# Probabilities loaded batch by batch, and the scaling of the joint slots' softmax on ScalarE

## The chip, the cores and the metric

The kernel runs on one core of a Trainium2 chip. The metric is the device time of one execution in microseconds (us). Three runs of the kernel before took 1032.5, 1033.79 and 1034.16 us; the median is 1033.79 us.

## What is computed

The inputs are q, k and v of 4 batches, 8 heads, 576 tokens and 64 columns, in fp32, a memory matrix and a vector for each batch and head, a gate for each head, and for each of the 2304 tokens four domain probabilities. In short:

```
scores = q @ k.T / 8, causal; a = softmax(scores)
phi(x) = max(x, exp(x) - 1 where x <= 0) + 1
x = g * (phi(q) @ M) / (phi(q) . z + 1e-6) + (1 - g) * (a @ v)      g = sigmoid(beta) per head
p = probs / (probs.sum(-1) + 1e-9)                                  per token, four experts
out = sum over e of p[:, e] * (relu(x @ w1[e]) @ w2[e])             512 -> 1024 -> 512
```

## The kernel before

**Tiles and stages.** Tokens are cut in chunks of 128 (the fifth chunk of a batch has 64). Chunks 0 and 1 of a batch are done together for a pair of heads ("joint" tasks), chunks 2 to 4 in tasks of their own. The expert part works on nine groups of 256 tokens. Group 0 is batch 0, chunks 0 and 1, which `first_run` computes alone at the start, in an order written out by hand (`ORDER`). After it the expert part runs in phases (half an expert each, 40 in all). A phase is four pieces of `mm1` (h = x·w1, four fc), each followed by relu into hh on ScalarE (L767) and the rest hl on VectorE (L768), then `mm2` (y = h·w2) for each tile of 128 tokens, whose result VectorE adds to acc with the token's probability as factor (L802, L804). Every fp32 product is three matmuls of rounded parts: high times high, and the two mixed ones. Phases 0 to 4 have one group, so 256 columns in mm1; from phase 5 on two groups share a phase (but in the last three), so 512 columns.

**Weights.** SyncE (SP) loads weight blocks into four buffers stg. `w_prep` makes the two parts of one block: the high part (w1h, or w2h) is copied by ScalarE at L205 for w1, and in phases 0 to 4 and the last four for w2 too; the low part (w1l, w2l) is a subtraction on GpSimd (POOL) at L209. When it is done the next block is loaded into the same buffer. Where a phase's mm1 piece has been evicted, w_prep makes one w2 block of the same phase; after each tile of mm2, w1 blocks of the next phase (two at a time in phases 0 to 4).

**Slots.** The attention of the other tasks is cut in steps with a slot number and a priority; sorted by these, they give one fixed list. A joint task has four slots. In its even slots it does the scores (`j_qk`: matmuls L421, mask and maximum L426 on VectorE), the exponentials with row sums (`j_exp`, L440, ScalarE) and the transposed probabilities of the slot before (`j_pt`: transposes L309, pth on ScalarE L480, ptl on VectorE L481). In its odd slots `j_norm` (priority -0.5, so the first of the slot) takes the two row sums (one per head), adds 1e-9 and multiplies with 1 + exp(beta) at L453, inverts at L456 and scales the exponentials at L458, all on VectorE. There are 24 joint slots; half have rows of 128 columns a head (chunk 0), half 256 (chunk 1).

Steps for tasks to come lie between. In a task's slot 1 (its first odd one) the queries of the next task are transposed (tq) and split: `split_q`, qa and qb on ScalarE (L317, L318), then the other halves on VectorE (L319, L322). In its last odd slot `t_phi1` does the ex operations of a task two ahead (L281, L282, ScalarE), and at the start of a task's first slot `t_trk` splits the next task's keys (kha, khb L329 on ScalarE, kl L331 on VectorE) and copies them across by DMA (`dup_k`, L336). At the end of a task's first slot `t_phi3` (L300 to L304, VectorE) normalises phi(q) of the next task and writes qp; in the task's second even slot `t_trqp` transposes its own qp (tp) and splits it (qpa, qpb).

**Order.** Each engine executes its instructions in the order in which the program issues them. How the list of steps is laid between the matmul pieces is a planner's choice: each step has a cost (400 without matmuls; 1500 and its matmul time with them), and before each mm piece steps are issued until their summed cost reaches a target that rises with the work done. The target is a line from the start to the steps that a group must have; it is steeper for the first groups.

**Probabilities.** `c_probs` (L729 to L738) is called once, in `first_run` after the weight step w3 and the steps up to slot -8. It loads the probabilities into the tile pn with eight DMAs of SP's queue: for each of four batches one of 8 KB (four full chunks) and one of 1 KB (the chunk of 64). `c_probs2` (L740 to L746, a step of slot -3 with priority 20) normalises all 18 columns of pn with four VectorE operations. Phase 0's first use of pn is the acc operation at L802.

Of the kernel before, what the change touches and what calls it, by code (L numbers as in the profile page):

```python
# [10 lines left out]
AF = mybir.ActivationFunctionType  # L11
ALU = mybir.AluOpType
AX = mybir.AxisListType
# [36 lines left out]
def tile_attention_moe(  # L50
# [13 lines left out]
    nc = tc.nc  # L64
    P = 128
    B, H, S, D = q.shape
    NT, DM = out.shape
    E, _, F = w1.shape
# [36 lines left out]
    def ctile(shape, dt, name):  # L105
        return cst.tile(shape, dt, tag=name, name=name)
# [15 lines left out]
    ebp = ctile([P, H], F32, "ebp")  # L122
    gate = ctile([P, H], F32, "gate")
    pn = ctile([P, NT // P, E], F32, "pn")
    psm = ctile([P, NT // P], F32, "psm")
# [65 lines left out]
    def w_prep(i, kind, pool=False):  # L191
        last_ = i >= PHASES - 4
        act = (kind == "1" or i < START[1] or last_) and not pool
        j = wpos["prep"]
        if j >= len(wseq) or wseq[j][0] != i or wseq[j][1] != kind:
            return
        wpos["prep"] += 1
        fc = wseq[j][2]
        t = stg.pop(j)
        hi, lo = (w1s if kind == "1" else w2s)[fc]  # L200
        if kind == "1":
            hi = hi.rearrange("p c f -> p (c f)")
            lo = lo.rearrange("p c f -> p (c f)")
        if act:
            nc.scalar.activation(hi, t, AF.Copy)  # L205
        else:
            nc.gpsimd.tensor_scalar(hi, t, 1.0, 1.0, ALU.mult, ALU.mult)  # L207
        dve = (last_ and fc % 2) or (i < START[1] and fc < PR["lod"])
        (nc.vector if dve else nc.gpsimd).tensor_tensor(lo, t, f(hi), ALU.subtract)  # L209
        w_dma()  # L210
# [179 lines left out]
    for t in tasks:  # L390
# [7 lines left out]
        for hds, c in order:  # L398
            s = Slot()
# [49 lines left out]
    def j_norm(i):  # L449
        s = slots[i]  # L450
        h = 2 * s.t.a
        r = s.st[:, 4:6]
        nc.vector.scalar_tensor_tensor(  # L453
            r, s.st[:, 2:4], 1e-9, ebp[:, h : h + 2], ALU.add, ALU.mult
        )
        nc.vector.reciprocal(r, r)  # L456
        for hd in range(2):
            nc.vector.tensor_scalar(  # L458
                s.s3[:, hd], s.s3[:, hd], r[:, hd : hd + 1], None, ALU.mult
            )  # L460

    def j_pt(i):
# [199 lines left out]
    def ev(slot, prio, fn, cost=0.0):  # L662
        events.setdefault(slot, []).append((prio, len(events.get(slot, [])), fn, cost))
# [21 lines left out]
    for i, s in slots.items():  # L685
        w = wid(s.c)
        t = s.t
        if t.joint:
            ev(i, PQ["qk"], lambda i=i: j_qk(i), 4 * mm(w))
            ev(i, PQ["exp"], lambda i=i: j_exp(i))  # L690
            ev(i + PQ["jn"][0], PQ["jn"][1], lambda i=i: j_norm(i))
            ev(i + PQ["jp"][0], PQ["jp"][1], lambda i=i: j_pt(i), 218.0 * (s.c + 1))
            if i in t.end:
                ev(i + PQ["jo"][0], PQ["jo"][1], lambda i=i: j_o(i), 6 * mm(GW) + 4 * mm(P))
            continue
        ev(i, PQ["qk"], lambda i=i: s_qk(i), 2 * mm(w) if w <= 512 else 6 * mm(w // 2))
        ev(i, PQ["exp"], lambda i=i: s_exp(i))
        ev(i + 1, PQ["norm"], lambda i=i: s_norm(i))
        ev(i + 2, PQ["pt"], lambda i=i: s_pt(i), 109.0 * min(s.c + 1, 4))
        if s.c == 4:  # L700
            ev(i + 2, PQ["pt"] + 0.1, lambda i=i: s_pt(i, True), 109.0)
        if i in t.end:
            cost = mm(t.nq) + sum(2 * mm(t.nq - max(0, j * P - t.q0)) for j in range(t.nk))
            ev(i + 3, PQ["o"], lambda i=i: s_o(i), cost)

    ev(-3, 20, lambda: c_probs2())
    steps = []
    for sl in sorted(events):
        es = sorted(events[sl], key=lambda e: (e[0], e[1]))
# [16 lines left out]
        b, c = pieces[0]  # L726
        return 4 * b + c if c < 4 else 4 * B + b // 2

    def c_probs():  # L729
        for b in range(B):  # L730
            nc.sync.dma_start(
                out=pn[:, 4 * b : 4 * b + 4],
                in_=probs[b * S : b * S + 4 * P].rearrange("(t p) e -> p t e", p=P),
            )
            nc.sync.dma_start(
                out=pn[(b % 2) * D : (b % 2) * D + D, 4 * B + b // 2],
                in_=probs[b * S + 4 * P : (b + 1) * S, :],
            )  # L738

    def c_probs2():  # L740
        nc.vector.tensor_reduce(psm, pn, AX.X, ALU.add)
        nc.vector.tensor_scalar(psm, psm, 1e-9, None, ALU.add)
        nc.vector.reciprocal(psm, psm)
        nc.vector.tensor_tensor(
            pn, pn, psm.unsqueeze(2).to_broadcast([P, NT // P, E]), ALU.mult
        )  # L746

    acc = {}
# [90 lines left out]
    def first_run():  # L839
        b = FIRST[0]  # L840
# [200 lines left out]
        def f_w(j):  # L1041
            w_prep(0, "1" if j < HF else "2", True)
            if j in (1, 3):
                while si[0] < len(steps) and steps[si[0]][0] <= (-9 if j == 1 else -8):
                    run_step()
            if j == 3:
                c_probs()

        def f_d(j):
            z_ = moe_bank(f"id{j}")  # L1050
# [26 lines left out]
        for j in range(2):  # L1077
            o = slice(j * D, (j + 1) * D)
            nc.sync.dma_start(out=mbd[o, :, o], in_=m4[j])
        nc.scalar.activation(ebp, betab, AF.Exp)  # L1080
        nc.scalar.activation(gate, betab, AF.Exp, scale=-1.0)
        nc.vector.tensor_scalar(ebp, ebp, 1.0, None, ALU.add)
# [41 lines left out]
    with tc.manual_schedule():  # L1124
        si = [0]

        def run_step():
            steps[si[0]][2]()
            si[0] += 1

        last_mask()
        for i in range(2):
            nc.gpsimd.memset(f(QK[i]["qz"]), 0.0)
            nc.gpsimd.memset(f(QK[i]["qa"][:, 3 * P :]), 0.0)
        first_run()
        phases = [phase_parts(i) for i in range(PHASES)]
        pcost = [sum(c for c, _ in ph) for ph in phases]
# [66 lines left out]
```

## Time and profile before

| | |
|---|---|
| three runs, median | 1033.79 us |
| the profiled execution | 1030.5 us |
| its span, first to last instruction | 1028.6 us |
| PE busy | 1006.3 us (98%) |
| VectorE (DVE) busy | 680.9 us (66%) |
| ScalarE (ACT) busy | 487.5 us (47%) |
| GpSimd (POOL) busy | 574.9 us (56%) |
| mean granted TensorE clock | 0.993 |

The profile is of one execution. Its own time, 1030.5 us, is 1.9 us more than its span and 3.3 us less than the median of the runs. The chain of work that ended last runs over PE for 87% of the span; the remaining PE idle time is 22 us. By slices of a fortieth of the span, PE's busy share is under 9 tenths only in the first, second, fourth and fifth (up to some 129 us) and the last. VectorE's is 8 tenths or more from the third to the eleventh, where the joint tasks run. A granted clock of 1.00 is 2.4 GHz, 0.50 is 1.2 GHz.

### The profile page before, as it was taken

What the parts mean: (1) busy time and instruction counts of PE and PEld (TensorE: products, weight loads), DVE (VectorE), ACT (ScalarE), POOL (GpSimd) and SP (SyncE); (2) the same over time, 40 slices, a digit from 0 to 9 for tenths busy, and PEclk for the clock granted to TensorE, in tenths of its full rate; (3) what the DMA queues carried; (4) which work ended last, traced back from release to release, by engine and by line L of the source; (5) the groups of instructions that cost most, each with busy time, mean ns of one, the idle gap of its engine ahead of it and who ended that gap; (6) DMA issues with size and microseconds to landing.
All of it is one profiled execution on the core that took longest, in us unless ns stands there. A gap on an engine that the chain in (4) does not pass through costs nothing.

```text
span 1028.6 us, 16265 instructions
## 1 busy us (share of the span) xinstructions
PE 1006.3 (98%) x5202; PEld 845.7 (82%) x5202; DVE 680.9 (66%) x1634; ACT 487.5 (47%) x1156; POOL 574.9 (56%) x557
## 2 busy tenths in 40 slices
PE   8798899999999999999999999999999999999998
PEld 5687788888888888888888888888888888888887
DVE  6588888888877776877687867766665323222344
ACT  7476756555555545544554555445444222211243
POOL 6476766666654465456554555565653645656233
PEclk9899999999999999999999999999999999999999
DMA  6566554464434444445434454353231432433254
GB/s 149 125 170 172 146 152 112 131 167 120 131 100 111 127 120 111 114 121 138 107 95 106 139 139 120 82 153 105 81 102 58 131 95 82 126 100 98 76 143 134
DMA packets 213669, 123.16 MB, mean 120 GB/s; under 512 B 100688, under 2 KB 187728, under 8 KB 213584
## 3 DMA queue, kind: packets, MB, share of 16 engines
q1 hardware_dynamic: 213440, 122.12, 44.0%
q8 instruction: 42, 0.69, 0.3%
q14 instruction: 43, 0.35, 0.1%
q10 hardware_dynamic: 144, 0.00, 0.0%
HBM read 106.86 MB, written 4.72 MB: 108 GB/s over the span
## 4 chain that ended last, share of the span: by engine, by line
PE 87%; DVE 4%; POOL 3%; issue 2%; ACT 1%; SPq 1%; DMA 1%; POOLq 0%; DVEq 0%; ACTq 0%
PE y L788 36%; PE h L758 35%; PE sp L547 4%; PE pt L309 4%; PE o L648 4%; POOL w1l L209 1%; POOL w2l L209 1%; PE tk L309 1%; PE tq L309 1%; PE tp L309 1%; PE sp L421 1%; PE o L495 0%; DMA kha<-kha 0%; ACT s L440 0%; PE o L643 0%
## 5 line engine op out<-in xcount | busy, mean ns | idle before, releaser
L209 POOL TENSOR_TENSOR w1l<-stg,w1h 128x512 fp32r<-128x512 f32 x152 | 198.4, 1317 | 315.4 <-ACT w1h L205 260.8
L758 PE MATMUL h<-xh,w1h 128*128 128x512 f32 (+1 forms) x640 | 248.0, 388 | 0.0
L758 PE MATMUL h<-xh,w1l 128*128 128x512 f32 (+1 forms) x640 | 237.3, 371 | 0.4 <-POOL w1l L209 0.4
L788 PE MATMUL y<-w2h,hh 128*128 128x512 f32 x576 | 237.6, 413 | 0.0
L758 PE MATMUL h<-xl,w1h 128*128 128x512 f32 (+1 forms) x640 | 236.3, 369 | 0.0
L788 PE MATMUL y<-w2h,hl 128*128 128x512 f32 x576 | 227.2, 394 | 4.2 <-DVE hl L768 4.2
L788 PE MATMUL y<-w2l,hh 128*128 128x512 f32 x576 | 226.5, 393 | 0.6 <-POOL w2l L209 0.6
L209 POOL TENSOR_TENSOR w2l<-stg,w2h 128x512 fp32r<-128x512 f32 x152 | 199.3, 1314 | 44.6 <-ACT w2h L205 34.0
L767 ACT ACTIVATE hh<-h 128x512 fp32r<-128x512 f32 (+1 forms) x160 | 88.9, 556 | 242.3 <-PE h L758 240.6
L768 DVE SCALAR_TENSOR_TENSOR hl<-h,hh 128x512 fp32r<-128x512 f32 (+1 forms) x160 | 101.9, 637 | 123.0 <-ACT hh L767 121.9
L804 DVE SCALAR_TENSOR_TENSOR acc<-y,pn,acc 128x512 f32<-128x512 f32 x126 | 94.3, 748 | 73.3 <-PE y L788 72.1
L758 PEld LDWEIGHTS h<-xh,w1l 128*128 128x128 f32 x640 | 120.8, 189 | 22.0 <-POOL w1l L209 0.6
L758 PEld LDWEIGHTS h<-xh,w1h 128*128 128x128 f32 x640 | 121.2, 189 | 16.3
L758 PEld LDWEIGHTS h<-xl,w1h 128*128 128x128 f32 x640 | 121.5, 190 | 15.7
L788 PEld LDWEIGHTS y<-w2h,hl 128*128 128x128 f32 x576 | 108.9, 189 | 30.3 <-DVE hl L768 6.1
L788 PEld LDWEIGHTS y<-w2l,hh 128*128 128x128 f32 x576 | 109.7, 190 | 19.0 <-POOL w2l L209 1.6
L788 PEld LDWEIGHTS y<-w2h,hh 128*128 128x128 f32 x576 | 109.3, 190 | 18.0
L590 ACT ACTIVATE pth<-pt 128x384 fp32r<-128x384 f32 (+3 forms) x128 | 50.6, 421 | 108.1 <-PE pt L309 107.7
L205 ACT ACTIVATE w1h<-stg 128x512 fp32r<-128x512 f32 x156 | 93.8, 625 | 9.6 <-DMA stg<-in_moe_w_dram 8.1
L207 POOL TENSOR_SCALAR w2h<-stg 128x512 fp32r<-128x512 f32 x128 | 82.0, 641 | 15.8 <-PE y L788 15.7
L309 PE MATMUL pt<-ident,s 128*128 128x128 f32 (+1 forms) x376 | 61.2, 274 | 0.4 <-DVE s L458 0.4
L555 DVE CUSTOM_DVE_ANT_0 s<-sp,mask 128x384 f32<-128x384 f32 (+1 forms) x96 | 52.9, 563 | 12.6 <-PE sp L547 11.8
(157 smaller groups left out, 1411.6 us busy)
## 6 DMA issues: line engine op xcount, KB each, us to landing
stg<-in_moe_w_dram SPq DMA_DIRECT2D x320, 256.0 KB, 2.9
natall<-in_k_dram SPq DMA_DIRECT2D x34, 128.0 KB, 2.8
out_dram<-acc SPq DMA_DIRECT2D x16, 256.0 KB, 2.0
natall<-in_v_dram SPq DMA_DIRECT2D x32, 128.0 KB, 2.5
natall<-in_q_dram SPq DMA_DIRECT2D x60, 64.0 KB, 2.7
kha<-kha SPq DMA_DIRECT2D x16, 128.0 KB, 3.0
khb<-khb SPq DMA_DIRECT2D x16, 128.0 KB, 2.6
natall<-in_k_dram SPq DMA_DIRECT2D x28, 64.0 KB, 2.4
```

Of the source, the lines that this page charges most:

```text
L205: nc.scalar.activation(hi, t, AF.Copy)
L207: nc.gpsimd.tensor_scalar(hi, t, 1.0, 1.0, ALU.mult, ALU.mult)
L209: (nc.vector if dve else nc.gpsimd).tensor_tensor(lo, t, f(hi), ALU.subtract)
L309: nc.tensor.transpose(dst, src, ident[0:n, 0:n])
L547: nc.tensor.matmul(pt[:, 0 : b_ - a], lhsT=q_, rhs=qk[k_][:, a:b_], start=y == 0, stop=y == len(pairs) - 1,)
L555: nc.vector.tensor_tensor_reduce(s.s[:, a:b_], pt[:, 0 : b_ - a], mask[:, m0 : m0 + b_ - a] if c < 4 else mask4[:, a:b_], 1.0, 3.0e38, ALU ...
L590: nc.scalar.activation(dh, src, AF.Copy)
L758: nc.tensor.matmul(pt[0][:, cols], lhsT=w_[:, c], rhs=x_[:, c, cols], start=(c == 0 and z == 0), stop=(c == NKD - 1 and z == 2),)
L767: nc.scalar.activation(h_, pt[0][:, cols], AF.Relu)
L768: nc.vector.scalar_tensor_tensor(l_, pt[0][:, cols], 0.0, f(h_), ALU.max, ALU.subtract)
L788: nc.tensor.matmul(pt[0], lhsT=h_[fc][:, tk], rhs=w_, start=(fc == 0 and z == 0), stop=(fc == HF - 1 and z == 2),)
L804: nc.vector.scalar_tensor_tensor(acc[g, tt], pt[0], pe, acc[g, tt], ALU.mult, ALU.add)
```

## The change

The scaling of the joint slots' exponentials (L458) goes from VectorE to ScalarE, in place in the program. The one operation on both row sums, which reads two tiles of two columns (L453), becomes two operations on one column each, with the head's factor as a per-row scalar operand. Batch 0's probabilities are loaded right after the memory matrices early in `first_run`, those of batches 1 to 3 in slots 2, 6 and 10, and the four short chunks in slot 14. The normalisation of pn is split: the four columns of batch 0 in slot -3, the other 14 columns in slot 16. Each of these is the last of its slot (priority 20). The five added steps have a planner's cost of 400 each. Nothing else is altered.

```diff
@@ j_norm
         r = s.st[:, 4:6]
-        nc.vector.scalar_tensor_tensor(
-            r, s.st[:, 2:4], 1e-9, ebp[:, h : h + 2], ALU.add, ALU.mult
-        )
+        for hd in range(2):
+            nc.vector.tensor_scalar(
+                r[:, hd : hd + 1],
+                s.st[:, 2 + hd : 3 + hd],
+                1e-9,
+                ebp[:, h + hd : h + hd + 1],
+                ALU.add,
+                ALU.mult,
+            )
         nc.vector.reciprocal(r, r)
         for hd in range(2):
-            nc.vector.tensor_scalar(
-                s.s3[:, hd], s.s3[:, hd], r[:, hd : hd + 1], None, ALU.mult
+            nc.scalar.activation(
+                s.s3[:, hd], s.s3[:, hd], AF.Copy, scale=r[:, hd : hd + 1]
             )
@@ list of steps
-    ev(-3, 20, lambda: c_probs2())
+    ev(-3, 20, lambda: c_probs2(0, 4))
+    for i, b in enumerate(range(1, B)):
+        ev(4 * i + 2, 20, lambda b=b: c_probs((b,)))
+    ev(14, 20, lambda: c_tails())
+    ev(16, 20, lambda: c_probs2(4, NT // P))
@@ loads and normalisation of pn
-    def c_probs():
-        for b in range(B):
+    def c_probs(bs):
+        for b in bs:
             nc.sync.dma_start(
                 out=pn[:, 4 * b : 4 * b + 4],
                 in_=probs[b * S : b * S + 4 * P].rearrange("(t p) e -> p t e", p=P),
             )
+
+    def c_tails():
+        for b in range(B):
             nc.sync.dma_start(
                 out=pn[(b % 2) * D : (b % 2) * D + D, 4 * B + b // 2],
                 in_=probs[b * S + 4 * P : (b + 1) * S, :],
             )
-    def c_probs2():
-        nc.vector.tensor_reduce(psm, pn, AX.X, ALU.add)
...
+    def c_probs2(c0, c1):
+        p_, m_ = pn[:, c0:c1], psm[:, c0:c1]
+        nc.vector.tensor_reduce(m_, p_, AX.X, ALU.add)
...
@@ first_run
-            if j == 3:
-                c_probs()
...
             nc.sync.dma_start(out=mbd[o, :, o], in_=m4[j])
+        c_probs((b,))
         nc.scalar.activation(ebp, betab, AF.Exp)
```

## Rows read from the trace of the kernel before

**Rows 1.** PE around 44 us: start, length, engine, line, what, [idle before, releaser].

```profile
43.96 0.44 PE L421 MATMUL sp<-kha,qa 128*128 128x128 f32 x1 [6.04 <-DMA kha<-kha]
```

**Rows 2.** Busy by stretch: PE, PEld, DVE, ACT, POOL (count); PEclk, DMA, GB/s.

```profile
44.00:49.20 5.20, 5.20 (x20) 4.69 (x21) 1.99 (x10) 1.44 (x6) 0.00 (x0) 0.50 0.02 4
...
52.31:68.66 16.35, 14.79 (x103) 12.95 (x101) 13.66 (x34) 12.18 (x32) 12.09 (x12) 1.00 0.59 162
...
86.80:90.20 3.40, 3.40 (x11) 2.62 (x10) 2.77 (x10) 2.82 (x9) 0.00 (x0) 0.50 0.63 187
...
125.00:1000.00 875.00, 873.94 (x4382) 733.12 (x4381) 574.74 (x1337) 392.41 (x900) 484.22 (x462) 1.00 0.42 114
```

**Rows 3.** SP's queue from 31 to 39 us, in order of time.

```profile
31.48 0.62 SPq L731 DMA_DIRECT2D pn<-in_moe_domain_probs_dram  x1
...
36.61 2.18 SPq L184 DMA_DIRECT2D stg<-in_moe_w_dram  x4
38.89 0.50 SPq L336 DMA_DIRECT2D kha<-kha  x1
```

**Rows 4.** ScalarE before the first joint scores.

```profile
34.00 0.38 ACT L329 ACTIVATE khb<-tk 64x256 fp32r<-64x256 f32 x1
```

**Rows 5.** PE's late matmuls in phases 1 to 4, in order of time.

```profile
68.18 0.50 PE L788 MATMUL y<-w2h,hl 128*128 128x512 f32 x1 [1.56 <-DVE hl L768]
...
85.53 0.51 PE L788 MATMUL y<-w2h,hl 128*128 128x512 f32 x1 [2.42 <-DVE hl L768]
...
102.80 0.50 PE L788 MATMUL y<-w2h,hl 128*128 128x512 f32 x1
...
117.95 0.66 PE L309 MATMUL tp<-ident,qp 128*128 128x128 f32 x2 [2.29 <-DVE qb L322]
```

**Rows 6.** ScalarE in the same phases, in order of time.

```profile
57.39 0.39 ACT L767 ACTIVATE hh<-h 128x256 fp32r<-128x256 f32 x1
...
60.28 0.40 ACT L440 ACTIVATE s<-s,st 128x128 f32<-128x128 f32 x1 [0.98 <-DVE st L426]
...
62.33 0.37 ACT L317 ACTIVATE qa<-tq 64x256 fp32r<-64x256 f32 x1
...
63.41 0.62 ACT L205 ACTIVATE w2h<-stg 128x512 fp32r<-128x512 f32 x1
...
72.17 0.41 ACT L281 ACTIVATE ex<-natall 128x256 f32<-128x256 f32 x1
...
73.73 0.38 ACT L767 ACTIVATE hh<-h 128x256 fp32r<-128x256 f32 x1
...
92.97 0.39 ACT L767 ACTIVATE hh<-h 128x256 fp32r<-128x256 f32 x1 [1.09 <-PE h L758]
...
108.41 0.38 ACT L767 ACTIVATE hh<-h 128x256 fp32r<-128x256 f32 x1 [0.27 <-PE h L758]
```

**Rows 7.** VectorE and POOL in the cycle of 57 to 73 us.

```profile
61.68 0.69 DVE L481 TENSOR_TENSOR ptl<-pt,pth 128x512 fp32r<-128x512 f32 x1 [0.88 <-ACT pth L480]
...
64.82 1.26 DVE L453 SCALAR_TENSOR_TENSOR st<-st,ebp 128x2 f32<-128x2 f32 x1
...
71.94 0.75 DVE L804 SCALAR_TENSOR_TENSOR acc<-y,pn,acc 128x512 f32<-128x512 f32 x1 [0.24 <-PE y L788]
...
60.78 5.29 POOL L209 TENSOR_TENSOR w2l<-stg,w2h 128x512 fp32r<-128x512 f32 x4
```

**Rows 8.** Single lines: count, duration in ns (least/median/most), first and last start.

```profile
L453 DVE SCALAR_TENSOR_TENSOR st<-st,ebp x24: 149/582/1264, 49.2 to 238.1; 128x2 f32<-128x2 f32 x24
...
L458 DVE TENSOR_SCALAR s<-s,st x48: 273/347/1559, 49.5 to 240.2; 128x128 f32<-128x128 f32 x24, 128x256 f32<-128x256 f32 x24
...
L584 DVE TENSOR_SCALAR st<-st,ebp x80: 198/205/211, 249.0 to 787.8; 128x1 f32<-128x1 f32 x80
...
L946 ACT ACTIVATE sf<-sf,stf x16: 387/448/508, 8.7 to 27.8; 128x128 f32<-128x128 f32 x8, 128x256 f32<-128x256 f32 x8
```

**Rows 9.** The operations of `c_probs2` in their stretch: DVE, ACT busy, PEclk, DMA, GB/s.

```profile
38.30:39.45 1.15, 0.90 (x4) 0.00 (x0) 1.00 1.09 329
```

More of the change, by code (lines that the diff above doesn't have):

```diff
@@ L738, in c_probs @@
             )
-    def c_probs2():
-        nc.vector.tensor_reduce(psm, pn, AX.X, ALU.add)
-        nc.vector.tensor_scalar(psm, psm, 1e-9, None, ALU.add)
-        nc.vector.reciprocal(psm, psm)
+    def c_probs2(c0, c1):
+        p_, m_ = pn[:, c0:c1], psm[:, c0:c1]
+        nc.vector.tensor_reduce(m_, p_, AX.X, ALU.add)
+        nc.vector.tensor_scalar(m_, m_, 1e-9, None, ALU.add)
+        nc.vector.reciprocal(m_, m_)
         nc.vector.tensor_tensor(
-            pn, pn, psm.unsqueeze(2).to_broadcast([P, NT // P, E]), ALU.mult
+            p_, p_, m_.unsqueeze(2).to_broadcast([P, c1 - c0, E]), ALU.mult
         )
```

## The prediction

> **What bounds the kernel now.** I read the busy times by stretch first, then what PE waited for, then the queues of the engines around each wait. Past 125 us PE is the bound: from 125 to 1000 it is busy for 873.94 of 875 us at a granted clock of 1.00 [rows 2]. A change can gain 1.1 us there and can lose more. The time to be had lies before: one wait of 6.04 us at 43.96 for the key copy kha [rows 1], after which 44.0 to 49.2 runs at a clock of 0.50 [rows 2], and once in each of phases 1 to 4 a late matmul, at 68.18, 85.53, about 102.8 and 117.95, with 1.56, 2.42 and 2.29 us before the first, second and fourth [rows 5]. The 2.42 too is followed by half clock, from 86.8 to 90.2 [rows 2]. The reader is to see that these are two different limits: the first is SP's queue, the others a ring through ScalarE, VectorE, POOL and PE.
>
> **The loads leave SP's queue.** The eight probability loads take SP from 31.48 to 36.61, 5.13 us, and the weight loads and kha stand behind them [rows 3]. Without them kha waits for its data, which ScalarE has at 34.38 [rows 4], so it goes at about 34.4, not 38.89. It took 43.96 - 38.89 = 5.07 us from issue to PE's start; with the same here PE starts at 39.5, 4.5 us earlier. The floor of the gain is 0 (the 1 MB of weights ahead of it land no sooner), the ceiling 6.04. I take 4.5, as the transfers ahead go out earlier with it. The wait left is 1.5 us; a wait of 1.56 lies in a stretch at 1.00 [rows 5, 2], so I also take back half of the 5.2 us at half clock, 2.6. Together -7.1 us.
>
> Batch 0's load is moved past SP's first weight loads, where I cost it at 0, and at 0.62 at most, its issue [rows 3]; it is needed only by the acc operation. The loads of batches 1 to 3 and the four short ones issue beside SP's weight loads of phases 0 to 3, which mostly wait for POOL; 0 us, and at most 7 x 0.62 = 4.3 if each delayed a copy that PE waits for (the row of kha shows that such a case exists). The split normalisation adds four operations in slot 16: 0.9 us as the four take now [rows 9], on VectorE, right before that slot's sums. I take 0.9 into cycle 4; the least is 0, the most 2.2 (each of two may wait as long as L453's longest, 1.26 less its least 0.15, but only one has POOL to wait for as a rule). The five steps add 2000 to the planner's sum before slot 18, some 2% of it; pieces shift by one matmul piece at most. 0 us, at most 1.5 either way (three y matmuls of 0.50 [rows 5]).
>
> **The sums and the scaling.** On VectorE L453 goes (24 of 149 to 1264 ns, median 582) for 48 like L584, which takes 198 to 211 ns in all 80 of its cases, and L458 goes, 48 of 273 to 1559 [rows 8]. So VectorE gets some 2 to 3 us back per task. That is worth nothing by itself unless VectorE ends the wait, so I ask who ends it after.
>
> ScalarE takes the scaling in its place in the program, ahead of the next qa (odd slot 1) and ahead of ex (odd slot 3). It must wait there for VectorE's reciprocal, and everything behind waits with it: hh, the w2h and w1h copies, so POOL's w2l, so PE. No row here shows this wait; I build it from rows of the cycle at 57 to 74 us. A pair of scalings is 0.7 us (128 columns) and 0.9 (256): one takes 0.387 to 0.508 [rows 8], and two lie between full overlap (0.4, 0.5) and end to end (0.8, 1.0); I am nearer the latter, since qa to the end of w2h, four operations, takes 64.03 - 62.33 = 1.7 without a gap [rows 6].
>
> *From hh to PE's late matmul.* ScalarE does hh, w2h, hh, w2h (2 x 0.9), the exponentials and the transposed block up to ptl: 61.68 - 60.28 = 1.4 [rows 6, 7]. From ptl to the sums VectorE takes 64.82 - 61.68 = 3.14 [rows 7]; the two new sums and the reciprocal 0.7 (three like L584 [rows 8]). ScalarE, free at 62.33 [rows 6], would stand until 65.5. Then the pair, 0.7, qa to w2h, 1.7, and POOL's last w2l, 5.29 / 4 = 1.32 [rows 7]. In all 1.8 + 1.4 + 3.14 + 0.7 + 0.7 + 1.7 + 1.3 = 10.7 us; before it was 68.18 - 57.39 = 10.8 [rows 5, 6]. So VectorE's gain is spent: PE now waits for w2l in place of hl.
>
> *From there to the next hh.* Before: 73.73 - 68.18 = 5.55 us [rows 5, 6]. After, ex starts not at 72.17 [rows 6] but behind acc (71.94, next operation 0.66 later, an estimate from 0.75 less the overlap), sums and reciprocal 0.7 and the pair 0.9: 74.2. That is +2.0 on all that follows.
>
> *Clock.* PE has 14.8 us of work in a cycle of 16.35 [rows 2]. With 2 us more it waits over 3, longer than the 2.42 that was followed by 3.4 us at half clock. PE is then later with the y that acc needs: +1.5 of the 1.7 lost in cycles that did not have it.
>
> The four cycles, PE's late matmul to the next:
> Cycle 1 (phase 0's slots 0 to 3, and up to 68.18) has both pairs, 1.6 us; the wait at the first, the 65.5 - 62.33 = 3.1 above less the ptl (0.7) that slot 0 has not, 2.4; the 0.7 of sums and reciprocal at the second; less the idle 0.98 before the exponentials at 60.28 [rows 6], which takes some of it up: hh comes 3.7 later against PE's own start, and hh to PE is 10.7 for 10.8: +3.6.
> Cycle 2: +2.0, +1.5 for the clock, and 10.7 for 85.53 - 73.73 = 11.8: +2.4.
> Cycle 3 (it had half clock already): 5.55 + 2.0 + 1.5 = 9.05 for 92.97 - 85.53 = 7.44, +1.6. In slot 12 the third hh stands behind the scaling too, with its w2h and the two evictions of o: 0.62 and three like the 0.37 of qa [rows 6], 1.7 more; one hh and w2h fewer, 0.9, lie before the exponentials, which I let wait 0.6 for the mask: 12.1 for 102.8 - 92.97 = 9.8, +2.3. Together +3.9.
> Cycle 4: +2.0, +1.5 for the clock; and up to tp, which waits for VectorE's qb: 1.5 and 1.4 to ptl, 3.14 to the sums, 0.9 of the split normalisation, sums 0.7, pair 0.7, qa and its partner on ScalarE 0.8, the same on VectorE 0.9 (an estimate): 10.0 for 117.95 - 108.41 = 9.5, +0.5. Together +4.0.
> Past 125 us ScalarE is busy for 392.41 of 875 us [rows 2] and copies no w2; I take the new waits as hidden by its idle time, and half of PE's 1.1 us of waits as gone: -0.5. If that cover fails, seven tasks by 1 us cost 7.
>
> Sum: -7.1 + 3.6 + 2.4 + 3.9 + 4.0 - 0.5 = +6.3 us. On the profiled execution's own 1030.5 us that is 1036.8; the median of the runs is 3.3 higher, which gives 1040.1.
>
> The Trainium skill bears on the first link. Perfetto Trace Analysis, section "Tensor Engine Instruction (MATMUL, LD_WEIGHTS)", calls ScalarE and VectorE strict FIFO. By that rule no copy behind the scaling can slip past it, and the sum stands; were it otherwise, the four cycles would cost nothing and -7.6 would be left. The rows so far show no operation that passes a waiting one.
>
> **Rivals.** *VectorE's relief is what counts* (faster). If ScalarE's stand is covered by the time in which it waits for PE anyhow, the waits of rows 5 shrink. All of them gone is -6.3, with their two half-clock stretches of 1.7 each -3.4; half of that with the -7.1 is -12, none of it -7.1; I take -8: 1026. For it: VectorE is the engine named at each of those waits, and L453 waits up to 1.1 us beyond its least. Against: w2l comes after the scaling, and ScalarE is busy 12.18 us of 16.35 in a cycle already. It decides if ScalarE stands under 1 us at the scaling.
> The Trainium skill, SBUF — State Buffer, section "SBUF: two separate sides", says that GpSimd and a VectorE operation of two SBUF inputs, or in a two-port mode, exclude each other for a whole instruction. By that rule the waits in L453 and L458 do go, and this rival gets its chance; rows 8 bear it out with L584's even 198 to 211 ns.
>
> *The clock holds.* The cycles lengthen but PE keeps full clock: without the 1.5 in cycles 2 to 4, 6.3 - 4.5 = +1.8: 1035.6.
>
> *The first gap stays.* kha lands no earlier, since the transfers ahead of it need the time: half of the 7.1 is lost, 6.3 + 3.5 = +9.8: 1043.6. For it: the transfer took 5 us for a small copy. Against: with the loads gone the weights ahead go out sooner.
>
> **Chances.** The forecast 0.50 (its own range 1036 to 1044), VectorE's relief 0.28, the clock holds 0.12, the first gap stays 0.10. A measurement of this kernel tells 0.2%, 2.1 us, from no change. Slower takes 0.47 of the forecast and all of the last, 0.57; within 0.2% the third, 0.12; faster the second and the forecast's tail, 0.31. The range goes from the relief's -8 to +12: 1026 to 1046, which leaves some 0.12 below and 0.07 above.
>
> **What would show it.** In the profile after, the wait before the first joint scores is 1 to 2 us and the stretch behind it at full clock (first step). ScalarE has idle time of some 3 us before the scaling in slots 4, 8 and 12, ended by VectorE's reciprocal (second). PE's waits in phases 1 to 4 end on POOL's w2l, not on hl, and are 3 us or more, with half clock after (third). Past 125 us PE's waits stay near 1 us. The prediction is wrong if ScalarE's idle time at the scaling is under 1 us, if PE's waits up to 125 us sum to less than before, or if the gap at the first scores is still 5 us.

## The result, and the profile after

The changed kernel takes 1039.8 us (median of 6 runs, 1038.4 to 1042.53), the kernel before in the same series 1033.97 us (6 runs, 1032.5 to 1035.12). The ratio is 1.0059, 95% interval 1.0043 to 1.0074: slower, where 1040.1 was forecast. The profiled execution took 1038.49 us, span 1036.6 us (before 1028.6), mean granted clock 0.997 (before 0.993). So the two profiles lie 8.0 us apart, the medians 5.8. PE is busy for 870.42 us between 125 and 1000 us (before 873.94 [rows 2]).

First the largest wait of any engine after, between 40 and 260 us (who waited, for whom: us in total, times, longest):

```profile
ACT s L464 <- DVE st L462: 49.2, 24, 4.1
```

It is new: ScalarE stands at each of the 24 pairs of scalings for VectorE's reciprocal, 2.05 us on average. PE's own waits over the whole span, same columns:

```profile
PE y L802 <- POOL w2l L209: 4.8, 5, 1.6
PE tk L309 <- DMA natall<-in_k_dram: 4.6, 4, 1.6
PE y L802 <- ACT w2h L205: 4.5, 3, 1.8
PE tp L309 <- DVE qb L322: 3.4, 2, 3.1
PE sp L421 <- DMA kha<-kha: 1.7, 1, 1.7
```

The wait for kha shrank from 6.04 us [rows 1] to 1.7. Where PE's mm2 waited for VectorE's hl [rows 5], it now waits for w2h and w2l, which stand behind the scaling on ScalarE and POOL. PE in order of time after; 39.74 answers to [rows 1], the y and tp lines to [rows 5]:

```profile
39.74 0.30 PE L421 MATMUL sp<-kha,qa 128*128 128x128 f32 x1 [1.67 <-DMA kha<-kha]
52.26 0.41 PE L309 MATMUL tk<-ident,natall 128*128 128x128 f32 x2 [1.59 <-DMA natall<-in_k_dram]
...
63.61 0.49 PE L802 MATMUL y<-w2h,hh 128*128 128x512 f32 x1 [1.12 <-ACT w2h L205]
64.98 0.50 PE L802 MATMUL y<-w2l,hh 128*128 128x512 f32 x1 [0.88 <-POOL w2l L209]
...
81.67 0.49 PE L802 MATMUL y<-w2h,hh 128*128 128x512 f32 x1 [1.58 <-ACT w2h L205]
83.03 0.50 PE L802 MATMUL y<-w2l,hh 128*128 128x512 f32 x1 [0.87 <-POOL w2l L209]
...
99.70 0.50 PE L802 MATMUL y<-w2h,hh 128*128 128x512 f32 x1 [1.80 <-ACT w2h L205]
101.06 0.51 PE L802 MATMUL y<-w2l,hh 128*128 128x512 f32 x1 [0.86 <-POOL w2l L209]
...
120.06 0.41 PE L309 MATMUL tp<-ident,qp 128*128 128x128 f32 x2 [3.06 <-DVE qb L322]
124.58 0.50 PE L802 MATMUL y<-w2l,hh 128*128 128x512 f32 x1 [1.57 <-POOL w2l L209]
```

The late matmuls of phases 1, 2 and 4 start at 64.98, 83.03 and 120.06, where before they started at 68.18, 85.53 and 117.95: 3.2 and 2.5 us ahead, then 2.1 us behind. At the end of the span PE is 8.0 us behind. So 5.9 us were lost past the fourth cycle. ScalarE around one stand, after (to be held against [rows 6]):

```profile
54.48 0.39 ACT L781 ACTIVATE hh<-h 128x256 fp32r<-128x256 f32 x1
...
57.60 0.63 ACT L205 ACTIVATE w2h<-stg 128x512 fp32r<-128x512 f32 x1
61.27 0.70 ACT L464 ACTIVATE s<-s,st 128x128 f32<-128x128 f32 x2 [3.03 <-DVE st L462]
61.87 0.36 ACT L317 ACTIVATE qa<-tq 64x256 fp32r<-64x256 f32 x1
...
62.93 0.62 ACT L205 ACTIVATE w2h<-stg 128x512 fp32r<-128x512 f32 x1
...
72.61 0.38 ACT L781 ACTIVATE hh<-h 128x256 fp32r<-128x256 f32 x1
```

ScalarE has nothing to do but wait for 3.03 us, while qa, hh and w2h stand behind. The w2h for which PE waits at 63.61 is the one that starts right after.

### The profile page after: what moved, and what is told of

The parts are those of the page before. It is cut to its first block, busy times and chain, and to the rows that moved or that the text cites. A ratio compares the mean times of both kernels' runs of the same rounds, so it can differ in the third digit from the quotient of the medians.

```text
span 1036.6 us, 16307 instructions
## 1 busy us (share of the span) xinstructions
PE 1007.7 (97%) x5202; PEld 843.9 (81%) x5202; DVE 652.9 (63%) x1614; ACT 503.7 (49%) x1204; POOL 572.1 (55%) x557
## 4 chain that ended last, share of the span: by engine, by line
PE 82%; issue 4%; POOL 4%; ACT 3%; DVE 3%; DMA 2%; SPq 1%; POOLq 0%; ACTq 0%; DVEq 0%
PE h L772 34%; PE y L802 34%; PE sp L553 4%; PE o L654 3%; PE pt L309 3%; POOL w2l L209 2%; POOL w1l L209 1%; PE tk L309 1%; DMA kha<-kha 1%; SPq L263 1%; PE tq L309 1%; PE tp L309 1%; ACT s L440 1%; DMA natall<-in_k_dram 0%; PE o L649 0%
## 5 line engine op out<-in xcount | busy, mean ns | idle before, releaser
L292 POOL TENSOR_TENSOR rl<-qp,zb 128x384 f32<-128x384 f32 (+1 forms) x28 | 25.1, 895 | 64.5 <-DVE qp L288 58.8
```

## The experiments

Every ratio is against the kernel before in runs of the same series. Its median was 1033.48 to 1034.48 us in these series, so a difference between kernels of different series is good to about 1 us. "In place" is the changed kernel's place for the scaling, right behind the sums and the reciprocal.

| scaling of the joint slots | loads of before | later loads |
|---|---|---|
| VectorE, sums of before | 1033.5 (the kernel before) | 1031.9 |
| VectorE, one-input sums | 1030.5 | 1030.5 |
| ScalarE, in place | 1046.6 | 1039.8 (the changed kernel) |
| ScalarE, later in the slot | 1026.9 | 1021.0 |

**The loads alone.** The later loads and the split normalisation with the sums and scaling of before:

```diff
 (changed kernel; j_norm as before the change)
-            nc.scalar.activation(s.s3[:, hd], s.s3[:, hd], AF.Copy, scale=r[:, hd : hd + 1])
+            nc.vector.tensor_scalar(s.s3[:, hd], s.s3[:, hd], r[:, hd : hd + 1], None, ALU.mult)
```

> The loads and the split normalisation as in the change, the sums and the scaling as before. Queue theory (ScalarE stands at the scaling and all behind it is late; the loads only gain): the wait before the first joint scores falls from 6.0 to 1.7 us and PE keeps the 4.2 to 4.9 us that the changed kernel has gained at its first tp, so 1028 to 1031 us. Rival (the moved loads and the split normalisation cost on the way what they gain at the start): 1033 to 1037 us, and the ScalarE part alone is harmless.

Measured: 1031.93 us, ratio 0.9989 (0.9977 to 1.0001). The wait for kha is down to 1.7 us as expected, but the gain of 2.5 to 5.5 us that the queue theory gives is not there: PE's later waits, in the columns used above, are

```profile
PE y L796 <- DVE hl L776: 6.1, 3, 2.8
PE tp L309 <- DVE qb L322: 4.7, 1, 4.7
```

against 4.2 and 2.3 us before. Against the kernel before PE is ahead by 6.4 us at the first tp and by 0.8 at the fifth (tp is the transpose of qp, done once a task; its starts serve as milestones below). Where VectorE ends PE's waits, PE started earlier only waits longer here.

**The normalisation alone.** The loads of before with the changed `j_norm`:

```diff
 (kernel before)
-            nc.vector.tensor_scalar(s.s3[:, hd], s.s3[:, hd], r[:, hd : hd + 1], None, ALU.mult)
+            nc.scalar.activation(s.s3[:, hd], s.s3[:, hd], AF.Copy, scale=r[:, hd : hd + 1])
```

> The sums and the scaling as in the change, the loads as before. Queue theory: PE loses what the changed kernel lost after its first tp, some 2 us in each of phases 1, 3 and 4 and 6 us past 125 us, on top of the kernel before: 1043 to 1048 us, with ScalarE standing some 45 to 50 us in all before the scaling. Rival (the relief of VectorE pays, and the loads are what costs): 1028 to 1034 us.

Measured: 1046.62 us, ratio 1.0124 (1.0109 to 1.0139), as the queue theory has it: the normalisation costs 13.1 us and the loads then bring 6.8. Part of both is clock: the mean granted clock is 0.988 to 0.989 in these runs and 0.992 to 0.998 in those of the changed kernel.

**The sums alone.** The kernel before with the two one-input sums, scaling on VectorE:

```diff
 (kernel before)
-        nc.vector.scalar_tensor_tensor(r, s.st[:, 2:4], 1e-9, ebp[:, h : h + 2], ALU.add, ALU.mult)
+            nc.vector.tensor_scalar(r[:, hd : hd + 1], s.st[:, 2 + hd : 3 + hd], 1e-9, ebp[:, h + hd : h + hd + 1], ALU.add, ALU.mult)
```

> Only the sums are changed (two operations on one column each in place of one on two columns); the scaling stays on VectorE, the loads as before. If the wait inside the sums operation is one with POOL that an operation of one input does not have, each sum takes 0.2 us, the late hl of phases 1, 2 and 4 come up to 1 us sooner, and the time is 1 to 3 us less: 1031 to 1033 us. Rival (the wait moves on to the scaling, which waits with POOL as well): the scaling's mean grows by what the sums lose, 1034 us.

Measured: 1030.53 us, ratio 0.9973 (0.9959 to 0.9988): a little faster, and somewhat more than expected. The sums are not what costs.

**A scaling that waits for nothing.** The changed kernel with the factor 1.0, which leaves the rows unnormalised:

```diff
-                s.s3[:, hd], s.s3[:, hd], AF.Copy, scale=r[:, hd : hd + 1]
+                s.s3[:, hd], s.s3[:, hd], AF.Copy, scale=1.0
```

> The changed kernel with the scaling on ScalarE by the constant 1.0 in place of the reciprocal, so the rows are left unnormalised: ScalarE does the same work in the same place but waits for nothing there. Queue theory (the wait costs, not the work): ScalarE's stand before the scaling goes, PE's waits for w2h and w2l go with it, 1027 to 1032 us. Rival (ScalarE's added work of some 1.5 us a task is what costs): 1037 to 1040 us, PE's waits as in the changed kernel.

Measured: 1022.27 us, ratio 0.989 (0.9877 to 0.9902). ScalarE does the same operations in the same place, so its work is not what costs; without the wait for the reciprocal the time is 17.5 us less. This is more than expected; the run with the later place on VectorE, below, prices VectorE's relief at 7.3 us, which would then be kept. The constant also frees the transposes, which read the scaled rows, from the reciprocal; the next run keeps that link.

**The same scaling, later.** Sums and reciprocal stay; the scaling is a step of its own at the end of the slot, with nothing added to the planner's sum:

```diff
+    def j_scale(i):
...
             ev(i + PQ["jn"][0], PQ["jn"][1], lambda i=i: j_norm(i))
+            ev(i + PQ["jn"][0], 8, lambda i=i: j_scale(i), -PR["wpe"])
```

> The changed kernel with the scaling issued later in ScalarE's program: not right behind the sums, but at the end of the same slot, behind the next task's qa and qb (slots 1 of a task) or behind ex and its exponential (slots 3). Same operations, same engines. Queue theory (what costs is that ScalarE stands at the scaling for VectorE's reciprocal, with qa, hh and the w2 copies behind it): by then the reciprocal is long done, ScalarE's idle time before its scalings falls from 49 us (24 of them) to under 15, the copies keep their times, and most of the 17.5 us between the changed kernel and the one with a constant scale come back: 1024 to 1031. Chain theory (what costs is that exponential, sums, reciprocal, scaling and transposes now cross between two engines, so that the transposes are late wherever the scaling stands): the scaling ends no earlier, the transposes wait for it, 1037 to 1042.

Measured: 1021.01 us, ratio 0.9878 (0.9859 to 0.9896). The fastest of all, faster than the queue theory's range and far from the chain theory's. ScalarE's idle time before the scalings is 17.7 us (just over the 15 that were named). ScalarE there, for the task of the rows above:

```profile
57.79 0.38 ACT L317 ACTIVATE qa<-tq 64x256 fp32r<-64x256 f32 x1
...
58.88 0.62 ACT L205 ACTIVATE w2h<-stg 128x512 fp32r<-128x512 f32 x1
60.81 0.69 ACT L468 ACTIVATE s<-s,st 128x128 f32<-128x128 f32 x2 [1.31 <-DVE st L462]
```

qa, hh and w2h go without a gap and w2h starts at 58.88, not 62.93; ScalarE still stands for 1.31 us, but nothing that PE needs soon is behind it. PE has no wait between 41.36 and 84.42 us.

**The later place, on VectorE.** The kernel just described with the scaling on VectorE:

```diff
-            nc.scalar.activation(s.s3[:, hd], s.s3[:, hd], AF.Copy, scale=r[:, hd : hd + 1])
+            nc.vector.tensor_scalar(s.s3[:, hd], s.s3[:, hd], r[:, hd : hd + 1], None, ALU.mult)
```

> The kernel with the later scaling, but with that scaling on VectorE: the place is the later one, the engine that of the kernel before. It tells whether the 1021 us come from the place or from VectorE's relief. Relief (VectorE ends the waits up to 125 us, and its 26 us of scalings only change their place in its queue): 1028 to 1033, as with the scaling on VectorE at its first place (1030.5). Place (qa, qb, the residuals and hl no longer stand behind the scaling, whichever engine does it): 1020 to 1025.

Measured: 1028.26 us, ratio 0.9946 (0.9927 to 0.9964): the value of the relief theory. The place brings 2.2 us on VectorE (against 1030.5), but the two intervals overlap; the engine brings 7.3 us more. So the rival of the prediction, that VectorE's relief counts, is true once the copies that PE needs no longer stand behind the wait.

**Later still.** The scaling in the next even slot, right ahead of the exponentials and the transposes:

```diff
-            ev(i + PQ["jn"][0], 8, lambda i=i: j_scale(i), -PR["wpe"])
+            ev(i + 2, 6.3, lambda i=i: j_scale(i), -PR["wpe"])
```

> The scaling on ScalarE later still: in the next even slot, between the qpa and qpb copies and the next exponentials, right ahead of the transposed block. ScalarE's idle time before its scalings (17.7 us in the kernel with the later scaling) should fall under 6. If that idle time still costs PE, 1017 to 1020; if the reciprocal is early enough already and the rest is hidden, 1020 to 1022; if the transposes now wait for the scaling (PE or its weight loads waiting for L468), 1023 to 1028.

Measured: 1035.43 us, ratio 1.0021 (1.0007 to 1.0035): the third case, and worse than its range. ScalarE's idle time before the scaling falls to 0.3 us, but the transposes now wait:

```profile
PE pt L309 <- ACT s L468: 11.2, 13, 1.5
```

The place has two sides: behind the copies that PE needs next, and well ahead of the transposes that read it.

**Early slots alone, and late slots alone.** The changed kernel with ScalarE's scaling in slots 0 to 15 (up to some 125 us) and VectorE's in the others, and its mirror:

```diff
+            if i < 16:     (the mirror: if i >= 16)
                 nc.scalar.activation(s.s3[:, hd], s.s3[:, hd], AF.Copy, scale=r[:, hd : hd + 1])
+            else:
+                nc.vector.tensor_scalar(s.s3[:, hd], s.s3[:, hd], r[:, hd : hd + 1], None, ALU.mult)
```

> The changed kernel with the scaling on ScalarE in slots 0 to 15 alone (up to about 125 us) and on VectorE, as in the kernel before, in slots 16 to 46. It tells where the 5.9 us come from that were lost past 125 us. Queue theory (each scaling costs where it stands, there too): 1032 to 1035, and the milestones past 125 us stop moving. Rival (those 5.9 us follow from the early lateness, or from the loads and the split normalisation that now lie there): 1038 to 1041, as in the changed kernel.

Measured: 1038.11 us (10 runs, 1034.63 to 1039.94), ratio 1.0035 (1.002 to 1.005): the rival's number, though the milestones past 125 us do stop moving, as the queue theory says (+8.05 us at the fifth tp, +8.17 at the last group of them). Both were wrong on the early part: in this profile PE loses 13.1 us between the first and the fifth tp, for 7.0 in the changed kernel's, with the same program up to slot 15. Of these 6.1 us some 3.4 are clock, by the granted clock from 50 to 65 us: 0.88, 0.50 and 0.94 in the three stretches of 5 us, 1.00 in the changed kernel. The rest are longer waits, as 4.67 us at the fifth tp for 3.06. The ten runs show the clock too: the two with a mean of 0.995 and 0.997 took 1034.63 and 1035.38 us, the eight with 0.991 to 0.993 took 1036.71 to 1039.94. PE and its stretches here (busy, count, PEclk, DMA, GB/s):

```profile
54.45 0.66 PE L309 MATMUL tk<-ident,natall 128*128 128x128 f32 x2 [2.34 <-DVE st L462]
```

```profile
50.00:55.00 5.00, 1.78 (x9) 0.88 0.48 109
55.00:60.00 5.00, 5.00 (x25) 0.50 0.81 236
```

> The mirror of the kernel with ScalarE's scaling in slots 0 to 15: the changed kernel with the scaling on VectorE in slots 0 to 15 and on ScalarE in slots 16 to 46. It tells what the scalings past 125 us cost by themselves. By the profile of the changed kernel (5.9 us lost past 125 us, none in its mirror): 1035 to 1037. By the medians (1039.8 for all, 1038.1 for slots 0 to 15, 1030.5 for none), if costs add: 1030.5 + 1.7 = 1031 to 1033.5.

Measured: 1033.91 us (12 runs, 1031.07 to 1038.48), ratio 1.0007 (0.9989 to 1.0024), just above the range by the medians and below that by the profile. Against 1030.5 without any scaling on ScalarE the early slots cost 7.6 us, the late ones 3.4, both together 9.3. PE's busy time from 125 to 250 us, in the columns of [rows 2], is here, in the changed kernel, and with the scaling on VectorE throughout (the next run):

```profile
125.00:250.00 125.00, 120.61 (x626) 98.63 (x626) 86.55 (x248) 79.33 (x209) 74.31 (x81) 1.00 0.50 131
```

```profile
125.00:250.00 125.00, 121.17 (x629) 99.21 (x628) 85.84 (x248) 79.46 (x210) 74.38 (x81) 1.00 0.50 131
```

```profile
125.00:250.00 125.00, 123.79 (x657) 103.65 (x656) 103.74 (x283) 71.38 (x186) 77.93 (x86) 1.00 0.52 137
```

So the late stands cost PE 2.6 to 3.2 us there, whatever the early slots did.

**Loads and sums.** The changed kernel with the scaling back on VectorE:

```diff
-            nc.scalar.activation(s.s3[:, hd], s.s3[:, hd], AF.Copy, scale=r[:, hd : hd + 1])
+            nc.vector.tensor_scalar(s.s3[:, hd], s.s3[:, hd], r[:, hd : hd + 1], None, ALU.mult)
```

> The changed kernel with the scaling back on VectorE throughout: the later loads and the one-input sums alone. Queue theory: no ScalarE wait, the two gains add: 1031.9 (loads alone) and 1030.5 (sums alone) against 1033.5 make 1029; with VectorE relieved by the sums the ring before 125 us may also keep more of the 5 us that the loads bring at first, so 1025 to 1030. Rival (the loads cost past 40 us what they gain, and the sums' gain is part of the same wait on VectorE, so that they do not add): 1030.5 to 1033.

Measured: 1030.52 us, ratio 0.9969 (0.9954 to 0.9984): the rival, at the low end of its range. The loads add nothing that shows to the sums; PE gives its early start back to VectorE, most of all here:

```profile
96.53 0.50 PE L802 MATMUL y<-w2h,hl 128*128 128x512 f32 x1 [2.14 <-DVE hl L782]
...
115.44 0.66 PE L309 MATMUL tp<-ident,qp 128*128 128x128 f32 x2 [4.25 <-DVE qb L322]
```

**Old loads with the later scaling.** The loads of before in the fastest kernel:

```diff
-    ev(-3, 20, lambda: c_probs2(0, 4))
...
+    ev(-3, 20, lambda: c_probs2())
...
+            if j == 3:
+                c_probs()
```

> The later scaling on ScalarE with the one-input sums, but with the probability loads of the kernel before. It tells what the loads are worth once neither ScalarE's stand nor VectorE's queue takes their gain back. If the 5 us at the first joint scores are then kept: 1021 + 5 = 1025 to 1028. Rival (they are given back in any case, as beside the kernel before's own sums and scaling, where they brought 1.5 us): 1020.5 to 1023.

Measured: 1026.94 us, ratio 0.9933 (0.9913 to 0.9953). Here the loads are worth 5.9 us, as expected: with VectorE relieved and ScalarE not standing, the early start is kept.

**The key loads ahead of qz.** In the changed kernel PE's transposes of keys wait 4.6 us for the k load. SP in order of time:

```profile
46.59 0.46 SPq L355 DMA_DIRECT2D qz<-qa  x1
47.17 0.52 SPq L355 DMA_DIRECT2D qz<-qb  x1
47.80 1.32 SPq L263 DMA_DIRECT2D natall<-in_q_dram  x2
49.19 0.97 SPq L263 DMA_DIRECT2D natall<-in_k_dram  x2
```

The qz copies wait for ScalarE's late qa and qb, and the loads stand behind them; the trial issues the loads first:

```diff
-        ev(ld, 8, lambda t=t: t_load(t))
+        ev(ld, 6.4, lambda t=t: t_load(t))
```

> The changed kernel with the q, k and v loads of a task issued ahead of the transposes of q in the same slot (priority 6.4 in place of 8), so that on SP they stand before the qz copies, not behind them. If the waits of PE's key transposes for the k load (4.6 us in all in the changed kernel) are a cost of its own, laid on by SP's queue behind the late qb, they go: 1034 to 1037. Rival (PE's next wait, for w2l or for VectorE's qb, takes their place, since ScalarE stands as before): 1038.5 to 1041.

Measured: 1042.57 us, ratio 1.0086 (1.007 to 1.0102): no gain, and both theories missed it on the high side. PE's waits there:

```profile
PE y L802 <- POOL w2l L209: 5.9, 6, 1.6
PE y L802 <- ACT w2h L205: 4.7, 3, 2.1
...
PE tk L309 <- DMA natall<-in_k_dram: 0.9, 1, 0.9
```

The wait for k falls from 4.6 to 0.9 us and those for w2l and w2h grow by 1.3, as the rival has it. Its mean clock is 0.993 for the changed kernel's 0.997, at most some 4 us of the span (0.992 or 0.993 in all six runs, for 0.992 to 0.998); why the clock fell more often there was not settled.

## Why the prediction was right, and which of its sizes were not

**Loads.** PE's first joint scores were forecast at 39.5 us after a wait of 1.5 us; they are at 39.74 after 1.67. SP's weight loads go at 31.68, kha at 34.14 (forecast 34.4):

```profile
31.68 2.35 SPq L184 DMA_DIRECT2D stg<-in_moe_w_dram  x4
34.14 0.54 SPq L336 DMA_DIRECT2D kha<-kha  x1
```

The term of -7.1 us is -6.8 by the runs with the changed normalisation, clock included, and -5.9 with the later scaling. That it would be 0 to 1.5 beside VectorE's own scaling, the prediction did not need and did not see. The full clock behind the wait did not come: the first 5 us run at 0.66. The stretch that the prediction took it from [rows 2] ends half a microsecond behind its wait, so it showed little of the clock that follows. By the first late matmul start, clock and cycle 1 make -3.5 us forecast, -3.2 measured, but by two errors that cancel. From the first joint scores to the first tp PE takes 7.54 us for 8.22 before, so the clock gave back 0.7 us, not 2.6; from there to the first late matmul it takes 17.70 us for 16.00, so cycle 1 cost 1.7 us, not 3.6.

**ScalarE's stand.** Forecast 3.1 us in slot 4, measured 3.03 (2.97 and 3.26 in slots 8 and 12); hh to the late matmul 10.7 us forecast, 64.98 - 54.48 = 10.5 measured; from there to the next hh +2.0 forecast, 72.61 - 64.98 = 7.63 for 5.55, +2.1, measured. PE's waits end on w2h and w2l, where w2l alone was named. The cost of the normalisation, +3.6 + 2.4 + 3.9 + 4.0 - 0.5 = +13.4 us, is +13.1 by the runs with the loads of before. That the stand is the cause is shown twice, by the constant factor (1022.3) and by the later place (1021.0). The Trainium skill, Perfetto Trace Analysis, section "Tensor Engine Instruction (MATMUL, LD_WEIGHTS)", calls these engines strict FIFO; no row of the 24 stands shows an operation that slips past the waiting one, and changing the place alone moved the time by 18.8 us.

**First size that was off: the clock in cycles 2 to 4, "+1.5" each.** I priced a wait of over 3 us in one piece, with half clock behind it. It comes in two pieces, 1.1 to 1.8 us for w2h and 0.9 for w2l, and the clock mostly holds. PE by stretches of 5 us (busy, count, PEclk, DMA, GB/s):

```profile
80.00:85.00 5.00, 2.55 (x13) 1.00 0.46 112
85.00:90.00 5.00, 5.00 (x37) 1.00 0.68 184
...
100.00:105.00 5.00, 4.14 (x11) 0.66 0.50 126
...
120.00:125.00 5.00, 3.37 (x16) 1.00 0.49 123
```

Cycle 2 measures +0.7 us for 2.4, cycles 3 and 4 together (32.42 to 37.03 us) +4.6 for 7.9. Without the three 1.5 the forecast was 0.9 and 4.9, so the other terms of these cycles were right in sum. In this profile the rival "the clock holds" is thus right up to 125 us; in the kernel with the scaling in the early slots alone the clock was lost, and the lateness at the fifth tp was 8.05 us for 2.1. With the loads of before and the changed normalisation it was lost as well: 0.90 in mean from 50 to 125 us, for 0.95 in the kernel before and 0.98 in the changed one. So the term was wrong for this execution, not for every start.

**Second size that was off: "the new waits as hidden", -0.5 us past 125 us.** The cover failed, and the prediction had named 7 us for that: 5.9 was measured from profile to profile, 3.4 by the medians of the late slots alone. 15 of the 24 stands lie past 125 us, 30.9 us together, up to 3.4 each. PE's busy time over 125 to 1000 us, in the columns of [rows 2]:

```profile
125.00:1000.00 875.00, 870.42 (x4340) 727.53 (x4339) 555.46 (x1320) 400.99 (x925) 481.26 (x460) 1.00 0.41 114
```

It is 3.5 us less than before. With the wait at 124.58 this leaves under 1 us that I could not assign. ScalarE's idle share of over half did not tell whether its queue is free at the moment when PE needs it. One link was not foreseen at all: late qa and qb hold SP's qz copies and with them the next key load. The two errors, -4.5 and +6.4, nearly cancel. What they leave, 8.0 us from profile to profile for 6.3 forecast, is taken up by the step from the profile to the median: 3.3 us were added for it, and in the changed kernel it is 1.3. The mechanism was right; that the time came out within 0.3 us was in good part luck.

**The rivals.** VectorE's relief was to decide "if ScalarE stands under 1 us at the scaling". Where it does so in mean, at the later place (17.7 us over 24 scalings, 0.74 each, the longest 2.8), the time is 1021 us, below the 1026 that I gave it. At the place of the change it does not, and this rival did not come true. The first gap did not stay: 1.67 us of 6.04 are left.

## What to carry to other kernels

Before an operation goes to an idle engine, ask what it waits for at its place in that engine's queue, and who needs what stands behind it: here the same 48 operations cost 9.3 us right behind their input and bring 9.5 a few places later (1039.8 and 1021.0 against 1030.5 us), and cost 4.9 again right ahead of their reader (1035.4). An early start is only worth what the next engine in the ring lets through: the loads brought 0 to 1.5 us beside VectorE's scaling and 5.9 without it. That an engine is busy for under half of the time does not show that a wait in its queue is covered: ScalarE was, and of its 49.2 us of stands 17.5 came out of the time when the wait was taken away.

## What the runs showed of the hardware that was not expected

The granted clock does not follow from the length of one wait alone in these rows: half clock stands behind 2.34 us at 54.45 in the kernel with the early slots alone, full clock behind 3.06 us at 120.06 in the changed kernel. After the wait for kha, 1.67 us in the changed kernel and 1.71 in the one with the loads alone, the stretch from 40 to 45 us has 0.66 in the first and 1.00 in the second. The changed kernel and the one with the key loads ahead of qz have a mean clock of 0.997 and 0.993.

The one-column sums are as even as those of [rows 8], on VectorE (duration least, median and most in ns):

```profile
L454 DVE TENSOR_SCALAR st<-st,ebp x48: 197/204/207, 45.0 to 246.7; 128x1 f32<-128x1 f32 x48
```

But one input alone does not make an operation even. VectorE's second normalisation has a one-input operation over 14 columns, here in the kernel with loads and sums; POOL's subtractions of the same time stand below it:

```profile
110.18 1.04 DVE L756 TENSOR_SCALAR psm<-psm 128x14 f32<-128x14 f32 x1
```

```profile
107.16 4.04 POOL L209 TENSOR_TENSOR w2l<-stg,w2h 128x512 fp32r<-128x512 f32 x3
```

It ends at 111.22, as POOL's subtractions end (111.20); in the changed kernel, with POOL idle since 115.97, the same operation at 116.42 takes 0.18 us. The Trainium skill, SBUF — State Buffer, section "SBUF: two separate sides", has GpSimd and a VectorE operation in a two-port mode exclude each other for a whole instruction; these rows would fit it if this operation runs in such a mode, which no row shows.
